# Earlier sinks for the second batch, first keys on a second queue, first query planes on two engines, wide masks behind them

## The chip, the cores and the metric
One core of one Trainium2 chip. The metric is device time in microseconds. The engines are TensorE (PE in the rows; PEld is its weight load), VectorE (DVE), ScalarE (ACT), GpSimd (POOL) and SyncE (SP), which here only issues DMAs. Each engine works through its own instructions in order.

## The reference
Sliding-window attention with four sink keys, and behind it a gated MLP with a short convolution:

```
scores = q @ k.T / 8;  keep = (key < n_sink) | (0 <= query - key < window)      # B=4, H=8, S=768, D=64
x   = softmax(where(keep, scores, -1e9)) @ v          # n_sink = 4, window = 128; heads joined: 512 columns
h   = relu(x @ w_in)                                  # 1024 columns
out = (h * sigmoid(conv3(h, conv_w))) @ w_out         # conv over the sequence, per column
```

q, k and v are float32; the MLP's weights come as float64, two words a number.

## The kernel before, in words
A short prelude loads the two scalars (number of sinks, window), starts the first loads, builds an identity and the tables of positions, and computes a flag; then all engines branch on it (L904 to L906). What follows is the fast path, `banded`; nothing of it starts before the branch.

Two heads make a pair `g`; four pairs make a batch of the input. A step `i` is one tile of 128 queries of one pair: 6 steps a pair, 24 a batch. The first batch goes in half pairs of three steps, in plain float32: `prep32` (L349) transposes three query tiles and three key tiles of the pair on TensorE; ScalarE writes the queries twice, as plane 0 and plane 1 (each with one head's rows scaled and the other's zero, by `headscale`), and then the keys. From the second batch on `prep` (L295) splits queries and keys into a high and a low part in the narrower matmul type; the low parts are staged in tiles of the tag "nat" (three buffers, `pieces_of`) and copied to their places by DMAs: `X<-bq` for queries, `kk<-bk` and `kk<-kk` for keys.

In each step `scores` multiplies (L378, or L381 and L382), VectorE adds the mask and takes the maximum (L577), ScalarE exponentiates (L580), VectorE sums and inverts (L583, L584), GpSimd scales (L586). One step later `transp` transposes the weights; later still `pv` multiplies them with v (L655) and adds the sinks' part (L678). Masks: `m0` for the first tile; `w1` and `w2` (wide, 260 columns) for the others of the first batch; `m1` and `m2` (narrow, 132 columns), made from the wide ones in `narrow_masks` (L484), for the later batches.

The sinks' values of the first batch lie in `c.vs`, inside a buffer of the keys, cleared by GpSimd behind the wide masks (L496) and loaded by `sink_load` (L416). Those of the later batches are fetched by `sink_fetch` (L426) into a "nat" tile, split by `sink_split` (L435: one instruction on ScalarE, three on VectorE) and copied to `vsr` by DMAs, two `vsr<-sink` and two `vsr<-vsr`. The fetch is written at a batch's first step, the split three steps later (L748 to L752).

The MLP's weights are fetched piece by piece (`wi_0r`, ..., also "nat" tiles), put together from their two words and split into two parts on ScalarE, VectorE and GpSimd (L118 to L131), all within the first batch. The MLP of a batch is cut into pieces that fill TensorE between the steps of the next one (L204 and L239).

A scheduler with its own cost model sets the order on each engine when the program is built. What is written inside `first` has a higher priority: scores, transposes, products and the preparation of later pairs. `follow` adds a dependence on another instruction. SyncE issues all DMAs but the very last.

Of the kernel before, what the change touches and what calls it, by code (L numbers as in the profile page):

```python
# [17 lines left out]
P = 128  # L18
D = 64
NEG = 1.0e9  # L20
NS = 4
# [45 lines left out]
class Moe:  # L67
# [31 lines left out]
    def load(self, src, name):  # L99
        nc, (rows, n) = self.c.nc, src.shape  # L100
        if src.dtype == F32:
            raw = self.mp.tile([P, 512], F32, tag="nat", name=f"{name}r", bufs=3)[0:rows, 0:n]
            nc.sync.dma_start(raw, src)
        else:
            raw = self.mp.tile([P, 512, 2], I32, tag="nat", name=f"{name}r", bufs=3)[0:rows, 0:n]
            nc.sync.dma_start(raw.rearrange("p n w -> p (n w)"), src.bitcast(I32))
        return raw
# [166 lines left out]
class Attn:  # L274
# [74 lines left out]
    def prep32(self, g, half, s, kk, tag, ahead):  # L349

        c, nc, T, HTL, kw = self.c, self.nc, self.T, self.HTL, self.kw
        tiles = slice(HTL * half, HTL * half + HTL)

        def turn(nm):
            pt = self.mps.tile([P, HTL, P], F32, tag=tag, name=f"tr{nm}{g}{half}", bufs=3 if tag == "h" else 2)
            for t in range(HTL):
                c.pin(nc.tensor.transpose(pt[:, t, :], s.raw[nm, half][:, t].rearrange("p a d -> p (a d)"), c.ident))
            if nm == "q":
                s.X[half] = f(self.ap.tile([P, 2, HTL, P], F32R, tag="X", name=f"X{g}{half}", bufs=3))
                for j in range(2):  # L360
                    self.evac(s.X[half][:, j], pt, c.headscale[:, j:j + 1])
            else:
                s.kk = kk
                self.evac(kk[:, tiles, 0:P], pt, 1.0)
                if half == 0:
                    nc.scalar.copy(kk[:, :, P:kw], kk[:, 0:1, 0:kw - P].to_broadcast([P, T, kw - P]))
            ahead()

        s.plain = True
        return [lambda nm=nm: turn(nm) for nm in "qk"]  # L370
# [19 lines left out]
        nc.vector.tensor_tensor(out=xL[:, hp, s], in0=px, in1=f(xH[:, hp, s]), op=ALU.subtract)  # L390


def load(c, g, nm, t, lo, hi):

    b, hp = divmod(g, c.H // 2)
    both = getattr(c, nm)[b, 2 * hp:2 * hp + 2]
    if nm == "v" and hi - lo == c.S // P:
        c.nc.sync.dma_start(t.rearrange("p j t d -> p (j t) d"), both.rearrange("j (t p) d -> p (j t) d", p=P))
        return t
    for j in range(2):  # L400
        c.nc.sync.dma_start(t[:, j] if nm == "v" else t[:, :, j], both[j].rearrange("(t p) d -> p t d", p=P)[:, lo:hi])
    return t


def load_half(c, g, nm, half, slot):
    n = c.S // P // 2
    return load(c, g, nm, slot, n * half, n * half + n)


def load_v(c, g, slot, lo=0, hi=None):  # L410
    hi = hi or c.S // P
    load(c, g, "v", c.v_raw[slot][:, :, lo:hi], lo, hi)
    return c.v_raw[slot]
# [37 lines left out]
def banded(c):  # L451
# [18 lines left out]
    nc.vector.tensor_tensor(out=m0, in0=inw, in1=sk, op=ALU.max)  # L470
    nc.vector.tensor_scalar(m0, m0, -NEG, NEG, ALU.mult, ALU.add)
    w1, w2 = wide
    nc.vector.tensor_scalar(w1[:, KW:SW], inw, -NEG, NEG, ALU.mult, ALU.add)
    nc.vector.tensor_scalar(w1[:, 0:P], prv, -NEG, NEG, ALU.mult, ALU.add)
    nc.vector.tensor_tensor(out=w1[:, P:KW], in0=sk[:, 0:NS], in1=prv[:, 0:NS], op=ALU.is_gt)
    nc.vector.tensor_scalar(w1[:, P:KW], w1[:, P:KW], -NEG, NEG, ALU.mult, ALU.add)
    nc.vector.tensor_copy(w2, w1)
    masks = nc.vector.tensor_scalar(w2[:, P:KW], sk[:, 0:NS], -NEG, NEG, ALU.mult, ALU.add)

    def afterwards(ins):  # L480
        c.tc.add_manual_dep(ins.ins, masks.ins.name, mybir.DependencyInfo(mybir.DependencyClass.Sync,
                                                                          mybir.DependencyReason.DATA), reason="masks")
# [1 line left out]
    def narrow_masks():  # L484
        for mk, w in ((m1, w1), (m2, w2)):
            ins = nc.scalar.copy(mk[:, 0:NS], w[:, P:KW])
            c.tc.add_manual_dep(ins.ins, c.turned.ins.name, mybir.DependencyInfo(mybir.DependencyClass.Sync,
                                                                                mybir.DependencyReason.DATA), reason="late")
            nc.vector.tensor_tensor(out=mk[:, NS:KW], in0=w[:, 0:P], in1=w[:, KW:SW], op=ALU.min)

    n0, n1 = T * KW, 3 * NPAIR * P
    A.zeros = m.room[0][:, 6 * SW:6 * SW + n0]
    afterwards(nc.gpsimd.memset(A.zeros, 0.0))
    kks = [f(ap.tile([P, 4, T, KW], F32R, tag="kk", name=f"kks{i}")) for i in range(2)]
    c.vs = kks[1].rearrange("p a t k -> p (a t k)")[0:6 * SP, 2 * n0:2 * n0 + n1].rearrange("p (u n) -> p u n", u=3)
    afterwards(nc.gpsimd.memset(c.vs, 0.0))  # L496
    vsr = cp.tile([3 * SR, 3, NPAIR * P], F32R, name="vsr")

    half_row = n1 // 2
# [210 lines left out]

    for x in prep(0):
        x()
    load_v(c, 0, 0, 0, T // 2)
    m.fetch(1)
    sink_load(c, 0)
    fetch()
# [17 lines left out]
    for i in range(NST + DL):  # L734
        if i < NST:
# [9 lines left out]
            if i == NSTB // 2:  # L745
                for x in range(0, 2 * half_row, half_row):
                    nc.sync.dma_start(f(vsr).rearrange("p u n -> p (u n)")[:, x:x + half_row], A.zeros[0:3 * SR, 0:half_row])
            if t == 0 and g and g % NPAIR == 0:  # L748
                sinks = sink_fetch(c, m, g // NPAIR)
                after = i + 3  # L750
            if i == after:
                sink_split(c, vsr, *sinks)  # L752
# [103 lines left out]
def attention_gated_mlp(ctx: ExitStack, tc: tile.TileContext, q, k, v, n_sink, window, w_in, conv_w, w_out, out):  # L856
# [11 lines left out]
    c.raw = [c.whole[i // 2][:, T // 2 * (i % 2):T // 2 * (i % 2 + 1)] for i in range(RAWB)]  # L868
    c.v_raw = [con.tile([P, 2, T, D], F32, name=f"vraw{i}") for i in range(2)]
    for i in range(RAWB):  # L870
        load_half(c, i // 2, "qk"[i % 2], 0, c.raw[i])
    fl = con.tile([P, 2], F32, name="fl")
    flag = con.tile([1, 1], I32, name="flag")
    nc.vector.tensor_scalar(fl[:, 0:1], c.wnv, 1.0, None, ALU.is_ge)
# [67 lines left out]
```

## Time and profile before

| | |
|---|---|
| time, median of 3 runs | 474.92 us (474.6 to 476.47) |
| profiled execution: time, span | 473.48 us, 471.8 us |
| granted clock of TensorE, mean | 0.997 |
| PE busy | 444.6 us (94%), 3181 instructions |
| PEld busy | 388.3 us (82%) |
| DVE busy | 339.0 us (72%) |
| ACT busy | 321.3 us (68%) |
| POOL busy | 281.3 us (60%) |
| first key and query loads | 96 KB each transfer, two transfers a half |
| a piece of w_in or w_out | 512 KB |

The span runs from the first to the last instruction. Busy time is that in which an engine has an instruction in work; waiting for a semaphore is not counted. A row that ends in brackets tells how long the engine idled before it and what released it; the releaser is inferred and can be wrong where several semaphores are waited for.

### The profile page before, as it was taken

Reading aid. Unit: us, or ns where it says so; the run is one execution under the profiler, and the core shown is the slowest. Engines: PE = TensorE matmul, PEld = TensorE weight load, DVE = VectorE, ACT = ScalarE, POOL = GpSimd, SP = SyncE. Lnnn points to the kernel's source line nnn. Section 1 sums busy time; section 2 is a strip of 40 time slices with the busy share of each in tenths; the row PEclk is TensorE's granted clock in tenths of the full one; section 3 lists DMA queues with packets and bytes.
Section 4 is the critical chain, followed back from the end, with each engine's and each line's share of the span. In section 5 each row is a group of like instructions: output and inputs, shape, how many; then the busy total and the mean of one; then the engine's idle time right before and its main releaser. Section 6 shows DMA issues by size and latency. Waiting matters only on the chain.

```text
span 471.8 us, 10560 instructions
## 1 busy us (share of the span) xinstructions
PE 444.6 (94%) x3181; PEld 388.3 (82%) x3181; DVE 339.0 (72%) x1190; ACT 321.3 (68%) x1027; POOL 281.3 (60%) x557
## 2 busy tenths in 40 slices
PE   3898989898899999999999999999999999999994
PEld 3576768697798988898989898988989898998982
DVE  4799999758858668786766859685767663665562
ACT  4989957768867868785867767675857654554542
POOL 3474786626858658676755757667656671445340
PEclk9999999999999999999999999999999999999998
DMA  6888674388667472655273655545250101000001
GB/s 140 219 229 251 183 201 107 81 199 203 167 153 179 137 175 68 161 146 133 61 192 81 166 119 134 143 120 124 71 141 15 46 1 46 0 23 24 24 24 53
DMA packets 105851, 55.91 MB, mean 119 GB/s; under 512 B 83072, under 2 KB 98712, under 8 KB 105784
## 3 DMA queue, kind: packets, MB, share of 16 engines
q1 hardware_dynamic: 105640, 55.00, 45.5%
q8 instruction: 28, 0.46, 0.4%
q14 instruction: 39, 0.32, 0.2%
q10 hardware_dynamic: 144, 0.13, 0.1%
HBM read 28.17 MB, written 6.29 MB: 73 GB/s over the span
## 4 chain that ended last, share of the span: by engine, by line
PE 75%; DVE 11%; ACT 4%; POOL 3%; DMA 2%; issue 2%; DVEq 0%; POOLq 0%; ACTq 0%
PE ph L204 26%; PE po L239 25%; PE px L655 7%; PE sc L382 3%; PE sc L381 3%; PE pts L617 3%; PE px L678 2%; DVE stm L122 2%; PE tq L305 1%; PE tk L331 1%; DVE stm L123 1%; DMA kk<-bk 1%; DMA raw<-in_q_dram 1%; DVE roomH L577 1%; DVE roomL L577 1%
## 5 line engine op out<-in xcount | busy, mean ns | idle before, releaser
L239 PE MATMUL po<-woH,g 128*128 128x512 f32 x384 | 138.2, 405 | 1.5 <-POOL g L226 0.8
L204 PE MATMUL ph<-xH,wiH 128*128 128x258 f32 (+1 forms) x384 | 110.7, 288 | 0.0
L204 PE MATMUL ph<-xL,wiH 128*128 128x258 f32 (+1 forms) x384 | 109.6, 286 | 0.0
L204 PE MATMUL ph<-xH,wiL 128*128 128x258 f32 (+1 forms) x384 | 109.1, 284 | 0.0
L226 POOL TENSOR_SCALAR g<-t 128x256 fp32r<-128x256 f32 x94 | 44.3, 472 | 74.5 <-DVE t L219 50.6
L586 POOL TENSOR_SCALAR pe<-pe,sm 128x132 f32<-128x132 f32 (+1 forms) x144 | 62.8, 447 | 37.7 <-DVE sm L584 19.2
L239 PEld LDWEIGHTS po<-woH,g 128*128 128x128 f32 x384 | 69.4, 189 | 13.2 <-POOL g L226 1.7
L227 POOL TENSOR_TENSOR g<-t,g 128x256 fp32r<-128x256 f32 x94 | 74.5, 793 | 5.8
L239 PE MATMUL po<-woL,g 128*128 128x512 f32 x192 | 76.1, 396 | 0.0
L216 DVE SCALAR_TENSOR_TENSOR t<-hb,cw,t 128x256 f32<-128x256 f32 x96 | 53.8, 560 | 29.4 <-ACT t L215 28.9
L204 PEld LDWEIGHTS ph<-xH,wiL 128*128 128x128 f32 x384 | 72.8, 190 | 2.2
L204 PEld LDWEIGHTS ph<-xH,wiH 128*128 128x128 f32 x384 | 72.7, 189 | 2.0
L204 PEld LDWEIGHTS ph<-xL,wiH 128*128 128x128 f32 x384 | 72.7, 189 | 1.6
L580 ACT ACTIVATE pe<-pe,sm 128x132 f32<-128x132 f32 (+1 forms) x144 | 58.2, 406 | 14.4 <-DVE sm L577 12.8
L218 ACT ACTIVATE t<-t 128x256 f32<-128x256 f32 x96 | 40.1, 418 | 36.3 <-DVE t L217 35.9
L219 DVE SCALAR_TENSOR_TENSOR t<-t,hb 128x256 f32<-128x256 f32 x96 | 48.3, 504 | 15.1 <-ACT t L218 14.3
L215 ACT ACTIVATE t<-hb,cw 128x256 f32<-128x256 f32 x96 | 49.0, 511 | 12.4 <-POOL g L227 10.1
L217 DVE SCALAR_TENSOR_TENSOR t<-hb,cw,t 128x256 f32<-128x256 f32 x96 | 54.4, 567 | 4.0 <-POOL pe L586 0.5
L211 ACT ACTIVATE hb<-ph 128x258 f32<-128x258 f32 (+1 forms) x96 | 36.8, 384 | 17.4 <-PE ph L204 13.9
L577 DVE CUSTOM_DVE_ANT_0 pe<-sc,m 128x132 f32<-128x132 f32 (+1 forms) x144 | 39.8, 287 | 7.7 <-PE sc L382 6.9
L381 PE MATMUL sc<-kk,X 128*128 128x260 f32 (+1 forms) x144 | 42.3, 304 | 1.5 <-issue 1.1
L655 PE MATMUL px<-pT,vraw 128*64 128x128 f32 (+1 forms) x512 | 43.0, 317 | 0.0
(161 smaller groups left out, 896.1 us busy)
## 6 DMA issues: line engine op xcount, KB each, us to landing
X<-bq SPq DMA_DIRECT2D x96, 96.0 KB
vraw<-in_v_dram SPq DMA_DIRECT2D x16, 384.0 KB
out_dram<-stm SPq DMA_DIRECT2D x23, 256.0 KB
kk<-kk SPq DMA_DIRECT2D x24, 198.0 KB
raw<-in_k_dram SPq DMA_DIRECT2D x24, 192.0 KB
raw<-in_q_dram SPq DMA_DIRECT2D x24, 192.0 KB
kk<-bk SPq DMA_DIRECT2D x48, 96.0 KB
raw<-in_q_dram SPq DMA_DIRECT2D x16, 96.0 KB
```

The source lines that it names most:

```text
L204: self.latest = nc.tensor.matmul(u.h[:, 0:W], w[:, cc, ff * P:(ff + 1) * P], x[:, cc, t0:t1], start=(i == 0), stop=(i == len(prods) - 1))
L215: nc.scalar.mul(a, prev, cw[:, 0, ff:ff + 1])
L216: nc.vector.scalar_tensor_tensor(out=e, in0=this, scalar=cw[:, 1, ff:ff + 1], in1=a, op0=ALU.mult, op1=ALU.add)
L217: nc.vector.scalar_tensor_tensor(out=a, in0=nxt, scalar=cw[:, 2, ff:ff + 1], in1=e, op0=ALU.mult, op1=ALU.add)
L219: nc.vector.scalar_tensor_tensor(out=a, in0=e, scalar=1.0, in1=this, op0=ALU.add, op1=ALU.mult)
L227: nc.gpsimd.tensor_tensor(out=u.g[:, 1], in0=a, in1=f(u.g[:, 0]), op=ALU.subtract)
L239: ins = nc.tensor.matmul(po[:, 0:c.DM], u.g[:, a, tt * P:(tt + 1) * P], w[:, ff, :], start=(ff == 0 and i == 0), stop=(ff == NFF - 1 and i ...
L381: self.c.pin(self.nc.tensor.matmul(pc, X[:, j, u, :], kk[:, j, lo:hi], start=True, stop=False))
L577: nc.vector.tensor_tensor_reduce(out=pe[:, j, cols], in0=pc[:, P - at:SW][:, cols], in1=mk, op0=ALU.add, op1=ALU.min, scale=1.0, scalar=3. ...
L580: exp = nc.scalar.activation(pe[:, j, cols], pe[:, j, cols], AF.Exp, bias=sm[:, j:j + 1], scale=-1.0, accum_out=sm[:, 2 + 2 * j:3 + 2 * j])
L586: nc.gpsimd.tensor_scalar(pe[:, j, cols], pe[:, j, cols], sm[:, 8 + j:9 + j], 1.0, ALU.mult, ALU.mult)
L655: ins = nc.tensor.matmul(px[h][D * j:D * j + D, P * at:P * at + n], s.v[:, j, kt, :], pT, start=(h not in open_), stop=False, skip_group_c ...
```

## The change
Five edits. The prelude issues the four first half loads from two queues, queries from SyncE's and keys from ScalarE's, and the first value load directly behind them, before the branch instead of after the first preparation. In the first preparation VectorE, not ScalarE, writes the second query plane (`c.moved`). The six instructions that make the wide masks, and the two clears behind them, are made to follow that. The two narrow masks' VectorE instruction is made to follow a late transpose (`c.turned`), as its ScalarE one did before. The second batch's sinks are fetched at step 21 instead of 24, and so split at 24 instead of 27; those of the third and fourth batch stay.

```diff
             if nm == "q":
                 for j in range(2):
-                    self.evac(s.X[half][:, j], pt, c.headscale[:, j:j + 1])
+                    if g == half == 0 and j:
+                        c.moved = nc.vector.tensor_scalar(s.X[half][:, j], pt, c.headscale[:, j:j + 1], None, ALU.mult)
+                    else:
+                        self.evac(s.X[half][:, j], pt, c.headscale[:, j:j + 1])
...
-def load(c, g, nm, t, lo, hi):
+def load(c, g, nm, t, lo, hi, by=None):
+    by = by or c.nc.sync
...
-        c.nc.sync.dma_start(t[:, j] if nm == "v" else t[:, :, j], both[j].rearrange("(t p) d -> p t d", p=P)[:, lo:hi])
+        by.dma_start(t[:, j] if nm == "v" else t[:, :, j], both[j].rearrange("(t p) d -> p t d", p=P)[:, lo:hi])
...
-    nc.vector.tensor_scalar(w1[:, KW:SW], inw, -NEG, NEG, ALU.mult, ALU.add)
-    nc.vector.tensor_scalar(w1[:, 0:P], prv, -NEG, NEG, ALU.mult, ALU.add)
...
-    masks = nc.vector.tensor_scalar(w2[:, P:KW], sk[:, 0:NS], -NEG, NEG, ALU.mult, ALU.add)
...
-            nc.vector.tensor_tensor(out=mk[:, NS:KW], in0=w[:, 0:P], in1=w[:, KW:SW], op=ALU.min)
+            ins = nc.vector.tensor_tensor(out=mk[:, NS:KW], in0=w[:, 0:P], in1=w[:, KW:SW], op=ALU.min)
+            follow(c, ins, c.turned, "late")
...
-    afterwards(nc.gpsimd.memset(A.zeros, 0.0))
-    afterwards(nc.gpsimd.memset(c.vs, 0.0))
...
     for x in prep(0):
         x()
-    load_v(c, 0, 0, 0, T // 2)
+    follow(c, nc.vector.tensor_scalar(w1[:, KW:SW], inw, -NEG, NEG, ALU.mult, ALU.add), c.moved, "masks later")
+    follow(c, nc.vector.tensor_scalar(w1[:, 0:P], prv, -NEG, NEG, ALU.mult, ALU.add), c.moved, "masks later")
...
+    masks = nc.vector.tensor_scalar(w2[:, P:KW], sk[:, 0:NS], -NEG, NEG, ALU.mult, ALU.add)
+    afterwards(nc.gpsimd.memset(A.zeros, 0.0))
+    afterwards(nc.gpsimd.memset(c.vs, 0.0))
     m.fetch(1)
     sink_load(c, 0)
...
-            if t == 0 and g and g % NPAIR == 0:
-                sinks = sink_fetch(c, m, g // NPAIR)
+            if i == NSTB - 3 or t == 0 and g > NPAIR and g % NPAIR == 0:
+                sinks = sink_fetch(c, m, max(1, g // NPAIR))
                 after = i + 3
...
     for i in range(RAWB):
-        load_half(c, i // 2, "qk"[i % 2], 0, c.raw[i])
+        load_half(c, i // 2, "qk"[i % 2], 0, c.raw[i], nc.scalar if i % 2 else nc.sync)
+    load_v(c, 0, 0, 0, T // 2)
```

## Rows read from the trace of the kernel before

**Rows 1.** Busy us (instructions) by stretch: PE, PEld, DVE, ACT, POOL; clock, DMA share, GB/s.
```profile
42.00:84.00 42.00, 37.54 (x277) 31.07 (x277) 41.83 (x110) 32.26 (x90) 27.45 (x36) 1.00 0.63 170
...
90.00:108.00 18.00, 18.00 (x158) 16.26 (x157) 10.88 (x41) 13.48 (x43) 6.50 (x13) 1.00 0.81 194
108.00:114.00 6.00, 5.33 (x44) 5.02 (x44) 5.93 (x27) 5.52 (x22) 3.21 (x8) 1.00 0.97 230
...
120.00:126.00 6.00, 4.80 (x30) 3.85 (x29) 5.13 (x28) 4.40 (x19) 5.30 (x12) 1.00 0.47 141
126.00:456.00 330.00, 329.59 (x2384) 293.90 (x2382) 229.79 (x815) 220.55 (x719) 204.68 (x413) 1.00 0.39 99
```

**Rows 2.** The chain of waits at the start: start us, us, what.
```profile
8.27 4.86 DMA raw<-in_q_dram
...
13.62 0.87 PE trq L357 x3
```

**Rows 3.** SyncE's queue at the start, in order of time: start us, us, issue.
```profile
1.25 0.42 SPq L57 DMA_DIRECT2D sc_i<-in_window_dram  x1
...
6.66 0.91 SPq L401 DMA_DIRECT2D vraw<-in_v_dram  x2
7.68 0.42 SPq L106 DMA_DIRECT2D wi_0r<-in_moe_w_in_dram  x1
8.27 0.90 SPq L401 DMA_DIRECT2D raw<-in_q_dram  x2
```

**Rows 4.** The engines at the start, in order of time.
```profile
4.79 0.17 DVE L59 CAST sc_f<-sc_i 128x4 f32<-128x4 int32 x1 [2.78 <-DMA sc_i<-in_window_dram]
...
6.91 0.88 PE L357 MATMUL trq<-ident,raw 128*128 128x128 f32 x3 [6.91 <-SPq L938]
...
7.90 1.05 ACT L288 ACTIVATE X<-trq,headscale 128x384 f32<-128x384 f32 x2 [1.93 <-DVE roomH L474]
...
10.71 0.29 DVE L577 CUSTOM_DVE_ANT_0 roomH<-sc,m 128x128 f32<-128x128 f32 x1 [1.60 <-PE sc L378]
...
12.89 0.66 ACT L118 ACTIVATE stm<-wi_0r 128x512 f32<-128x512 f32 x1 [0.48 <-DMA wi_0r<-in_moe_w_in_dram]
...
14.51 1.05 ACT L288 ACTIVATE X<-trq,headscale 128x384 f32<-128x384 f32 x2 [0.47 <-PE trq L357]
```

**Rows 5.** Busy time by stretch again, the first loads.
```profile
4.50:7.00 2.50, 0.10 (x1) 0.13 (x2) 1.96 (x10) 0.20 (x1) 0.38 (x11) 1.00 1.07 241
```

**Rows 6.** The masks: roomH's instructions by stretch (DVE fourth); L489's durations.
```profile
7.33:9.20 1.87, 0.00 (x0) 0.00 (x0) 1.46 (x8) 0.00 (x0) 0.23 (x1) 1.00 0.82 136
...
L489 DVE TENSOR_TENSOR m<-roomH x2: 286/288/289, 8.0 to 8.8; 128x128 f32<-128x128 f32 x2
```

**Rows 7.** The sinks' tile alone, by stretch: DVE, ACT, clock, DMA share, GB/s.
```profile
108.00:114.00 6.00, 1.88 (x3) 0.60 (x1) 1.00 0.97 230
```

**Rows 8.** SyncE's queue at the second batch's start.
```profile
101.99 1.14 SPq L431 DMA_DIRECT2D sink<-in_v_dram  x3
...
112.53 0.54 SPq L344 DMA_DIRECT2D kk<-kk  x1
...
118.23 1.79 SPq L446 DMA_DIRECT2D vsr<-sink  x2
120.12 1.41 SPq L340 DMA_DIRECT2D kk<-bk  x2
121.63 1.67 SPq L448 DMA_DIRECT2D vsr<-vsr  x2
```

**Rows 9.** Who waited for whom, 90 to 127 us: us, times, longest.
```profile
PE tk L637 <- DVE sk L629: 0.7, 1, 0.7
...
PE sc L381 <- issue: 1.1, 1, 1.1
...
ACT kk L342 <- DMA kk<-bk: 1.6, 1, 1.6
```

**Rows 10.** ScalarE at the fifth pair's second query half.
```profile
96.66 0.50 ACT L288 ACTIVATE bq<-tq 128x384 fp32r<-128x384 f32 x1
```

More of the change, by code (lines that the diff above doesn't have):

```diff
@@ L400, in load, with load_half @@
     for j in range(2):
-        c.nc.sync.dma_start(t[:, j] if nm == "v" else t[:, :, j], both[j].rearrange("(t p) d -> p t d", p=P)[:, lo:hi])
+        by.dma_start(t[:, j] if nm == "v" else t[:, :, j], both[j].rearrange("(t p) d -> p t d", p=P)[:, lo:hi])
     return t
-def load_half(c, g, nm, half, slot):
+def load_half(c, g, nm, half, slot, by=None):
     n = c.S // P // 2
-    return load(c, g, nm, slot, n * half, n * half + n)
+    return load(c, g, nm, slot, n * half, n * half + n, by)
 def load_v(c, g, slot, lo=0, hi=None):
@@ L472, in banded @@
     w1, w2 = wide
-    nc.vector.tensor_scalar(w1[:, KW:SW], inw, -NEG, NEG, ALU.mult, ALU.add)
-    nc.vector.tensor_scalar(w1[:, 0:P], prv, -NEG, NEG, ALU.mult, ALU.add)
-    nc.vector.tensor_tensor(out=w1[:, P:KW], in0=sk[:, 0:NS], in1=prv[:, 0:NS], op=ALU.is_gt)
-    nc.vector.tensor_scalar(w1[:, P:KW], w1[:, P:KW], -NEG, NEG, ALU.mult, ALU.add)
-    nc.vector.tensor_copy(w2, w1)
-    masks = nc.vector.tensor_scalar(w2[:, P:KW], sk[:, 0:NS], -NEG, NEG, ALU.mult, ALU.add)
     def afterwards(ins):
@@ L712, in banded @@
         x()
-    load_v(c, 0, 0, 0, T // 2)
+    follow(c, nc.vector.tensor_scalar(w1[:, KW:SW], inw, -NEG, NEG, ALU.mult, ALU.add), c.moved, "masks later")
+    follow(c, nc.vector.tensor_scalar(w1[:, 0:P], prv, -NEG, NEG, ALU.mult, ALU.add), c.moved, "masks later")
+    follow(c, nc.vector.tensor_tensor(out=w1[:, P:KW], in0=sk[:, 0:NS], in1=prv[:, 0:NS], op=ALU.is_gt), c.moved, "masks later")
+    follow(c, nc.vector.tensor_scalar(w1[:, P:KW], w1[:, P:KW], -NEG, NEG, ALU.mult, ALU.add), c.moved, "masks later")
+    follow(c, nc.vector.tensor_copy(w2, w1), c.moved, "masks later")
+    masks = nc.vector.tensor_scalar(w2[:, P:KW], sk[:, 0:NS], -NEG, NEG, ALU.mult, ALU.add)
+    afterwards(nc.gpsimd.memset(A.zeros, 0.0))
+    afterwards(nc.gpsimd.memset(c.vs, 0.0))
     m.fetch(1)
```

## The prediction

> **What bounds the kernel now.** I read the table of busy time by stretch first. From 126 us to 456 us TensorE is busy in 329.59 of 330 us [rows 1]: whatever reaches 126 us sooner ends sooner by as much, and nothing behind 126 us can be won. Ahead of it TensorE idles 0 in 90 to 108 us, 0.67 us in 108 to 114 and 1.20 us in 120 to 126, and in 42 to 84 us it is VectorE that is full (41.83 of 42 us) [rows 1]. So there are two places to look at: the start, because what delays VectorE's first work delays the whole first batch, and the entry into the second batch at 108 to 126 us. The chain of waits, read second, says what ends the start: the third query load, 4.86 us after its issue, and then its transposes at 13.62 us [rows 2]. SyncE's queue, third, says why that load is late: the first value load (0.91 us of issuing) and the weight piece wi_0r are issued ahead of it, from 6.66 us on, when the branch into the fast path has been taken [rows 3]. The engines' rows, fourth, give the branch itself: VectorE reads the window size at 4.79 us after waiting for its load, TensorE begins at 6.91 us, and ScalarE evacuates the first query planes, two in 1.05 us, from 7.90 us [rows 4]. For the second batch I read SyncE's queue and the waits.
>
> **The loads.** Two key halves leave SyncE's queue for ScalarE's, and the value load moves ahead of the branch, right behind the queries. ScalarE has nothing but the table load and one tiny activation until 7.90 us, so four issues cost it nothing. On SyncE the block's first issue is then wi_0r, at 6.66 instead of 7.68 us: 1.02 us sooner [rows 3]. The third query load still needs its buffer, free when the first query transposes are done (6.91 + 0.88 = 7.79 us [rows 4]), so it is issued some 0.4 us sooner; but it stands behind the 512 KB of wi_0r on the same 16 DMA engines, so its landing follows wi_0r's. I take 1.0 us sooner at the transposes of 13.62 us. Can ScalarE use that? It now idles 0.48 us for wi_0r at 12.89 us [rows 4], and it gets work out of its way by the next part, so it can. The bounds are 0 (ScalarE, not the load, is late) and 1.5 us (0.52 us of work and its waits of 0.48 and 0.47 us [rows 4] all gone).
>
> A load added beside the two scalar loads can also cost. The window size was issued at 1.25 us and read at 4.79 us [rows 3, 4]; now keys come from a second queue to the same engines meanwhile. Four key transfers of 96 KB at the 241 GB/s that 4.5 to 7 us shows, with the engines full [rows 5], are 1.6 us: the flag, and with it everything behind the branch, could be that much later. Or 0, if its few packets are through before the keys'. I take 0.2 us, near the lower end: the queries issued right behind it from 1.71 us on shared the engines with it before, too. The Trainium skill, DMA: Bandwidth & Descriptors, "Issuing engines are not separate DMA queues", says that loads started by different engines interleave on the same 16 DMA engines and that a second issuer saves only the issuing time; no row here shows two queues at once, and by that rule alone the keys gain no bandwidth and the scalar loads do share.
>
> **The first planes.** The second of the two evacuations goes to VectorE: 0.52 us less on ScalarE, whose first key evacuation and first scores come that much sooner. VectorE has the room: it waits 1.60 us for the first scores at 10.71 us [rows 4]. This is not added to the 1.0 us; it lets ScalarE take that. If both planes were still done one behind the other, the buffer would be free at 9.0 us as now, and the second group's transposes would gain nothing.
> The Trainium skill, PSUM — Partial Sum Buffer, "PSUM bank collisions raise a hardware error", wants accesses of ScalarE and VectorE to one bank kept apart, reads too; no row here shows the two on one PSUM tile at once. By it the second plane would start behind the first, the start would gain some 0.8 us instead of 1.0, and the sum below would be 1.7 us.
>
> **The masks.** The wide masks move behind that evacuation: six instructions, which with the two narrow ones are 1.46 us busy [rows 6]. They fit into VectorE's 1.60 us wait, late by about 0.9 us, and so are the two clears behind them on GpSimd and the six sink loads on SyncE. Those loads are first read with the products of the first sinks, steps later; cost 0 to 0.9 us, taken 0 for that cover; if it were gone, those products would wait the 0.9 us. The two narrow masks (0.29 us each [rows 6]) are now tied to a late transpose and leave this idle stretch for the neighbourhood of 85 us, where VectorE is still the one behind: 0 to 0.58 us, taken 0.3.
>
> **The sinks of the second batch.** Fetch, split and copies move three steps ahead. In 108 to 114 us VectorE is busy 5.93 of 6 us [rows 1] and 1.88 us of it are the sinks' three instructions, with 0.60 us on ScalarE [rows 7]; three steps sooner, in 90 to 108 us, VectorE is busy 10.88 of 18 us [rows 1]. So that part is free where it goes. What it frees: TensorE's wait of 0.7 us for VectorE's sk [rows 9] should vanish, but what TensorE needs next is the sixth head pair's keys, whose last copies are issued at 112.53 us [rows 8] and which hang on the end of the first batch (the buffer), not on the sinks; TensorE then only waits there longer. I take 0.2 us of the 0.7 and of the 1.1 us for the scores behind it [rows 9], between all of it, 1.8, and nothing.
> On SyncE's queue the two vsr<-sink issues take 118.23 to 120.02 us, and the seventh pair's low keys, kk<-bk, issue at 120.12 [rows 8]; ScalarE then idles 1.6 us for them [rows 9], and TensorE's 1.20 us in 120 to 126 us follow. With the 1.79 us gone from there that wait and those gaps should be gone: 1.2 us. Bounds 0 (another transfer takes the place) and 1.2.
> Where they go, SyncE has them ahead of the sixth pair's keys: the fetch (1.14 us) leaves 101.99 us for the idle queue before, but copies of 1.79 and 1.67 us come in: 3.46 - 1.14 = 2.3 us more at worst ahead of 112.53 us [rows 8], 0 at best, if they fall into the hole that the fetch leaves and others like it. I take 0, nearer to it, because the copies that remain are split by a landing and need not stand together; the 0.2 above is net of it.
>
> **The sum.** 1.0 - 0.2 - 0.3 + 0.2 + 1.2 = 1.9 us less. The profiled execution took 473.48 us (span 471.8), so 471.6 us on its scale. It lies 1.44 us below the median shown, 474.92 us, so I forecast 474.92 - 1.9 = 473.0 us.
>
> **The rivals.**
> 1. All gaps of the second batch's entry close: 1.2 us and the whole 1.8 us instead of 0.2, and the start gains its 1.0 without the deductions: 1.2 + 1.8 + 1.0 = 4.0 us, 470.9 us. For it: VectorE and SyncE both get freer at 108 to 120 us. Against: the sixth pair's keys are a chain of transfers that the change does not shorten.
> 2. The entry gains nothing: the keys at 120 us wait for another issue in the place of vsr<-sink, and only the start is left, 0.5 us: 474.4 us. For it: from 118.23 to 123.30 us the queue has no hole [rows 8]. Against: ScalarE's wait of 1.6 us is just as long as the two issues.
> 3. Slower. The sinks share three buffers with the low parts of keys and queries. Fetched at about 85 us, they hold one until vsr<-sink has landed; the second query half of the fifth pair, evacuated by ScalarE at 96.66 us [rows 10], can be given that buffer. ScalarE works in order, so behind its wait stand the exponentials and the copies of transposes, and TensorE behind these. The sinks held their buffer 18 us, from 101.99 to 120.02 us [rows 8]; from 85 us that would be 103 us, a wait of some 6.4 us at 96.66. Less the gain of 1.9 us it is 4.5 us more: 479.4 us; it decides from a wait of 1.9 us on. Against: of three buffers the sinks may as well hold one that nobody wants until they are through; no row of before can show which.
> 4. The change's first part backfires: the flag is 1.6 us late by the keys' traffic. Then 1.9 - 1.4 = 0.5 us is left of the gain: 474.4 us, no slower.
>
> **Chances.** Forecast 0.44 (its own range 472.0 to 474.2, about a quarter of it below 472.5), rival 1 0.27, rivals 2 and 4 together 0.17, rival 3 0.12. What one measurement can tell here from no change is about 0.5%, 2.4 us: below 472.5 us is faster, above 477.3 slower. Faster: 0.27 and 0.11 of the forecast's, 0.38. Slower: most of rival 3, 0.10. The same: 0.52. The range goes from 470.2 us (rival 1 with another 0.5 us, up to the start's bound of 1.5, and 0.2 us for the spread of the runs) to 476.4 us (rival 3 with a wait of 3.4 us).
>
> **What would show it.** Right: wi_0r issued at 6.7 us, the third query's transposes at about 12.6 us, VectorE's plane beside ScalarE's; vsr<-sink issued before 110 us; no wait of ScalarE for kk<-bk at 123 us, and TensorE idle under 0.3 us in the 6 us around it. Wrong: TensorE's first transposes later than 7.2 us (the flag); ScalarE waiting before a query evacuation near 96 us (the buffer); or over 1.8 us of TensorE's idling before the sixth pair's first scores, which would mean that the sinks' copies stand in front of its keys.

## The result, and the profile after

The changed kernel is slower. It takes 478.99 us (median of 14 runs, 476.72 to 483.67) against 474.28 us for the kernel before (14 runs, 472.78 to 477.12): a ratio of 1.0105, with a 95% interval of 1.0079 to 1.0131. That is 4.7 us more, outside the predicted range. The profiled execution took 479.68 us with a span of 478.0 us. Of the runs of the experiments below, two slow ones (1523 us of e5, 480.9 us of e15) are left out of the ratios.

On the page of the changed kernel, the line of TensorE's busy time and, in 40 slices of 11.95 us, the clock that it was granted:

```profile
PE 448.7 (94%) x3181; PEld 390.4 (82%) x3181; DVE 339.3 (71%) x1191; ACT 320.3 (67%) x1026; POOL 279.9 (59%) x557
...
PEclk9989999998999999999999999999999999999998
```

The 3181 matmuls are the same as before, yet they keep TensorE busy for 4.1 us more than the 444.6 us of before. Three slices of the clock stand at 8: the last, as before, and the third and the tenth, which were at 9 before. The busy time by stretch (PE, PEld, DVE, ACT, POOL, then clock, DMA share, GB/s) shows it closer:

```profile
24.00:26.00 2.00, 1.84 (x4) 1.40 (x5) 1.49 (x7) 1.21 (x8) 2.00 (x5) 0.54 0.82 214
26.00:28.00 2.00, 2.00 (x21) 1.62 (x21) 2.00 (x8) 1.47 (x5) 1.10 (x2) 0.61 0.87 270
...
114.00:116.00 2.00, 0.21 (x2) 0.24 (x3) 0.92 (x3) 1.61 (x6) 0.00 (x0) 1.00 0.90 205
116.00:118.00 2.00, 2.00 (x12) 2.00 (x12) 1.63 (x9) 2.00 (x9) 1.18 (x3) 0.58 1.05 278
118.00:120.00 2.00, 2.00 (x12) 2.00 (x11) 1.30 (x5) 0.77 (x3) 1.92 (x4) 0.57 0.64 163
120.00:126.00 6.00, 6.00 (x43) 5.41 (x42) 4.02 (x16) 4.82 (x17) 4.66 (x11) 1.00 0.59 159
126.00:456.00 330.00, 327.04 (x2362) 290.72 (x2361) 231.16 (x829) 220.45 (x723) 202.39 (x413) 1.00 0.39 100
```

The clock stood at 1.2 GHz, half of 2.4, twice for 3.4 us, from 24.2 us and from 116.3 us; the second time right behind a stretch in which TensorE worked for 0.21 of 2 us. Matmuls for 6.8 us at half speed cost some 3.4 us. From 126 to 456 us TensorE idles for 2.96 us, against 0.41 before [rows 1].

TensorE's last matmul ends 5.5 us later than before. That is 4.1 us of busy time, 0.2 us of later start and, as the difference, 1.2 us of idling. The idling did not grow ahead of 126 us; the first two rows are of the kernel before, the others of the changed one:

```profile
0.00:126.00 126.00, 105.75 (x756) 87.40 (x757) 104.44 (x366) 96.21 (x300) 74.60 (x142) 1.00 0.69 179
108.00:126.00 18.00, 15.07 (x104) 13.10 (x104) 15.17 (x73) 14.50 (x56) 13.67 (x28) 1.00 0.69 176
```

```profile
0.00:126.00 126.00, 106.87 (x743) 87.80 (x744) 99.91 (x347) 92.55 (x287) 72.56 (x137) 0.97 0.67 178
108.00:126.00 18.00, 16.09 (x110) 15.18 (x109) 11.82 (x49) 13.44 (x49) 9.37 (x21) 0.91 0.77 193
```

Up to 126 us TensorE idles 1.1 us less than before (19.13 us for 20.25), and 1.0 us of that lies at the entry into the second batch (1.91 us for 2.93). So the profile's loss is 3.4 us of half clock, some 0.7 us of other busy time and 2.55 us of idling behind 126 us, less these 1.1 us.

The start, answering to [rows 3] and [rows 4] (start us, us, engine line, what, and in brackets the idle time before):

```profile
4.98 0.17 DVE L59 CAST sc_f<-sc_i 128x4 f32<-128x4 int32 x1 [2.96 <-DMA sc_i<-in_window_dram]
6.85 0.34 SPq L106 DMA_DIRECT2D wi_0r<-in_moe_w_in_dram  x1
7.10 0.87 PE L357 MATMUL trq<-ident,raw 128*128 128x128 f32 x3 [7.10 <-SPq L942]
7.31 0.36 SPq L106 DMA_DIRECT2D wi_1r<-in_moe_w_in_dram  x1
8.00 0.91 SPq L405 DMA_DIRECT2D raw<-in_q_dram  x2
8.10 0.58 ACT L288 ACTIVATE X<-trq,headscale 128x384 f32<-128x384 f32 x1 [1.94 <-DVE m L475]
8.78 0.62 DVE L362 TENSOR_SCALAR X<-trq,headscale 128x384 f32<-128x384 f32 x1 [0.71 <-ACT X L288]
...
12.90 0.65 PEld L357 LDWEIGHTS trq<-ident,raw 128*128 128x128 f32 x3 [0.32 <-ACT kks L369]
13.11 0.85 PE L357 MATMUL trq<-ident,raw 128*128 128x128 f32 x3
```

The second batch's start in SyncE's queue, answering to [rows 8]: first the sixth pair's keys in the kernel before, then the changed kernel, and below it the changed kernel's chain of waits over the same time:

```profile
106.18 3.02 SPq L340 DMA_DIRECT2D kk<-bk  x4
```

```profile
103.47 1.78 SPq L450 DMA_DIRECT2D vsr<-sink  x2
...
106.54 1.57 SPq L452 DMA_DIRECT2D vsr<-vsr  x2
...
110.12 3.19 SPq L340 DMA_DIRECT2D kk<-bk  x4
...
115.32 0.54 SPq L344 DMA_DIRECT2D kk<-kk  x1
...
122.51 1.28 SPq L340 DMA_DIRECT2D kk<-bk  x2
```

```profile
110.18 0.56 SPq L340
110.74 0.05 issue
110.79 3.50 DMA kk<-bk
114.29 0.02 issue
114.31 0.04 ACTq L342
114.35 0.04 issue
114.39 0.27 ACT kk L342
114.66 0.40 ACT bq L288
115.06 0.02 issue
115.08 0.57 DVE bq L310
115.65 0.14 issue
115.79 4.29 PE ph L204 x21
```

The sixth pair's keys (kk<-bk) are issued behind the sinks' copies, and the landing of these keys is what TensorE waits for: ScalarE, in order, can't evacuate the query behind its wait for kk, VectorE can't make bq, and TensorE stands still for 1.91 us until 115.79 us. What it then begins with are matmuls of the MLP (ph L204); the sixth pair's first scores come behind these. That is the last sign on the prediction's list of wrong ones. The waits of 90 to 127 us, answering to [rows 9], no longer have TensorE waiting for sk; ScalarE's wait for the keys is this one:

```profile
ACT kk L342 <- DMA kk<-bk: 2.2, 1, 2.2
```

### The profile page after: what moved, and what is told of

The parts are those of the page before. It is cut to its first block, busy times and chain, and to the rows that moved or that the text cites. A ratio compares the mean times of both kernels' runs of the same rounds, so it can differ in the third digit from the quotient of the medians.

```text
span 478.0 us, 10559 instructions
## 1 busy us (share of the span) xinstructions
PE 448.7 (94%) x3181; PEld 390.4 (82%) x3181; DVE 339.3 (71%) x1191; ACT 320.3 (67%) x1026; POOL 279.9 (59%) x557
## 4 chain that ended last, share of the span: by engine, by line
PE 76%; DVE 7%; ACT 5%; POOL 4%; issue 2%; DMA 2%; SPq 1%; POOLq 0%; ACTq 0%; DVEq 0%
PE ph L204 27%; PE po L239 26%; PE px L651 7%; PE sc L385 3%; PE sc L384 3%; PE pts L613 3%; PE px L674 2%; PE tk L331 1%; PE sc L381 1%; PE tq L305 1%; POOL roomH L582 1%; POOL roomL L582 1%; ACT stm L118 1%; DVE stm L122 1%; DMA kk<-bk 1%
## 5 line engine op out<-in xcount | busy, mean ns | idle before, releaser
L204 PE MATMUL ph<-xH,wiH 128*128 128x258 f32 (+1 forms) x384 | 112.6, 293 | 1.9 <-DVE bq L310 1.9
L204 PE MATMUL ph<-xL,wiH 128*128 128x258 f32 (+1 forms) x384 | 110.5, 288 | 0.0
L204 PE MATMUL ph<-xH,wiL 128*128 128x258 f32 (+1 forms) x384 | 110.2, 287 | 0.0
L226 POOL TENSOR_SCALAR g<-t 128x256 fp32r<-128x256 f32 x94 | 42.5, 452 | 69.2 <-DVE t L219 42.4
L216 DVE SCALAR_TENSOR_TENSOR t<-hb,cw,t 128x256 f32<-128x256 f32 x96 | 55.9, 583 | 36.2 <-ACT t L215 35.8
L204 PEld LDWEIGHTS ph<-xH,wiH 128*128 128x128 f32 x384 | 73.5, 191 | 4.2 <-issue 2.1
L227 POOL TENSOR_TENSOR g<-t,g 128x256 fp32r<-128x256 f32 x94 | 73.1, 778 | 5.5
L204 PEld LDWEIGHTS ph<-xH,wiL 128*128 128x128 f32 x384 | 73.4, 191 | 2.1
L204 PEld LDWEIGHTS ph<-xL,wiH 128*128 128x128 f32 x384 | 73.3, 191 | 1.7
L217 DVE SCALAR_TENSOR_TENSOR t<-hb,cw,t 128x256 f32<-128x256 f32 x96 | 50.7, 529 | 3.9 <-DVE t L216 0.5
L572 DVE COPY_PREDICATED sc<-before,sc 128x128 f32<-128x128 int32 x120 | 33.3, 289 | 17.4 <-PE sc L385 17.0
L617 POOL TENSOR_SCALAR_AFFINE_SELECT pT<-pT 128x256 f32<-128x256 f32 x60 | 27.1, 452 | 28.4 <-ACT pT L615 26.1
## 6 DMA issues: line engine op xcount, KB each, us to landing
raw<-in_k_dram SPq DMA_DIRECT2D x24, 192.0 KB
raw<-in_q_dram SPq DMA_DIRECT2D x24, 192.0 KB
```

The source lines that it names most:

```text
L204: self.latest = nc.tensor.matmul(u.h[:, 0:W], w[:, cc, ff * P:(ff + 1) * P], x[:, cc, t0:t1], start=(i == 0), stop=(i == len(prods) - 1))
L216: nc.vector.scalar_tensor_tensor(out=e, in0=this, scalar=cw[:, 1, ff:ff + 1], in1=a, op0=ALU.mult, op1=ALU.add)
L217: nc.vector.scalar_tensor_tensor(out=a, in0=nxt, scalar=cw[:, 2, ff:ff + 1], in1=e, op0=ALU.mult, op1=ALU.add)
L226: nc.gpsimd.tensor_scalar(u.g[:, 0], a, 1.0, 1.0, ALU.mult, ALU.mult)
L227: nc.gpsimd.tensor_tensor(out=u.g[:, 1], in0=a, in1=f(u.g[:, 0]), op=ALU.subtract)
```

## The experiments

All are compared with the kernel before in runs on the same chip (median 473.7 to 474.3 us). "Clock" is the mean granted clock over all runs of the kernel (0.996 for the kernel before, 0.990 for the changed one), "idle" TensorE's idle time in 126 to 456 us of its profile (before 0.41, changed 2.96 us). "List" tells which order of matmuls TensorE's list of instructions has from the program's 1200th matmul (in the trace at 212 us before) to the 2400th (388 us), where all lists meet again: a as before, b as in the changed kernel, c to f others; e10's list is d from 221 us on, and that of e14 and e16 is b from 250 us on. The order is made by the scheduler that builds the program (the planner, below), so an edit anywhere can give another list.

| | edit | us | ratio, 95% interval | clock | idle | list |
|-|-|-|-|-|-|-|
| e1 | sinks sooner | 477.4 | 1.0065, 1.0037 to 1.0093 | 0.994 | 1.78 | c |
| e2 | loads | 474.9 | 1.0009, 0.9989 to 1.0028 | 0.991 | 1.06 | d |
| e3 | planes, masks, tie | 478.6 | 1.0083, 1.0053 to 1.0113 | 0.993 | 2.80 | b |
| e4 | all but the sinks | 478.0 | 1.0073, 1.0040 to 1.0106 | 0.991 | 0.70 | a |
| e5 | planes, wide masks | 474.8 | 1.0022, 1.0000 to 1.0045 | 0.992 | 0.40 | a |
| e6 | tie alone | 480.2 | 1.0136, 1.0103 to 1.0168 | 0.992 | 1.88 | b |
| e7 | e1, copies by GpSimd | 477.7 | 1.0073, 1.0043 to 1.0102 | 0.997 | 4.45 | e |
| e8 | sinks fetched sooner | 474.3 | 1.0005, 0.9982 to 1.0028 | 0.996 | 0.41 | a |
| e9 | changed, split later | 480.7 | 1.0143, 1.0121 to 1.0165 | 0.986 | 0.77 | a |
| e10 | changed, tie sooner | 477.7 | 1.0081, 1.0053 to 1.0108 | 0.991 | 1.50 | d |
| e11 | e1, tie one step sooner | 476.1 | 1.0045, 1.0026 to 1.0064 | 0.993 | 0.86 | a |
| e12 | tie three steps sooner | 477.1 | 1.0064, 1.0049 to 1.0079 | 0.992 | 0.76 | a |
| e13 | e2, filled | 476.8 | 1.0046, 1.0024 to 1.0067 | 0.993 | 0.43 | d |
| e14 | narrow masks later, free | 474.4 | 1.0006, 0.9983 to 1.0029 | 0.997 | 0.75 | f, then b |
| e15 | e4 without tie, filled | 476.1 | 1.0025, 0.9997 to 1.0052 | 0.992 | 0.43 | d |
| e16 | e14 with the tie | 475.1 | 1.0033, 1.0009 to 1.0056 | 0.994 | 0.47 | f, then b |
| e17 | keys by ScalarE | 475.1 | 1.0014, 0.9994 to 1.0033 | 0.996 | 0.44 | a |
| e18 | parts that leave the list | 475.1 | 1.0025, 1.0004 to 1.0046 | 0.992 | 0.42 | a |

**The parts, e1 to e4.** e1 is the kernel before with the changed lines of the sinks; e2 with those of the loads; e3 with the second plane, the wide masks and the tied narrow masks; e4 is the changed kernel with the sinks at their old place.

```
 e1  -  if t == 0 and g and g % NPAIR == 0:
     +  if i == NSTB - 3 or t == 0 and g > NPAIR and g % NPAIR == 0:
 e2  +  load_half(..., nc.scalar if i % 2 else nc.sync); load_v(c, 0, 0, 0, T // 2)
 e3  +  c.moved = nc.vector.tensor_scalar(...); follow(c, <wide masks>, c.moved, ...)
     +  follow(c, ins, c.turned, "late")     (narrow masks)
 e4  the changed kernel with "if t == 0 and g and g % NPAIR == 0:"
```

> Before, with only the second batch's sinks three steps sooner. Theory K (the sinks' copies stand in SyncE's queue ahead of the sixth pair's keys; TensorE waits 1.9 us for them and its clock then falls to half for 3.4 us): the same wait near 115 us and the fall behind it, so 1.0 to 1.9 us of wait + 1.7 us of clock, less the 1.2 us gained behind: ratio 1.003 to 1.007. Theory S (the loss is made at the start, by the loads, planes and masks): no loss here, ratio 0.995 to 1.000. Theory P (any edit changes the order on all engines and so the fill of TensorE): a loss anywhere, TensorE idle spread over the later batches.

> Before, with only the loads moved (keys by ScalarE's queue, first values before the branch). K: the start gains up to 0.5 us, nothing lost: ratio 0.998 to 1.000. S: a fall of the clock near 24 us as in the changed kernel, 1.7 us, ratio 1.003 or more. P: a loss with another order, idle spread.

> Before, with only the second query plane on VectorE and the masks behind it (wide and narrow). K: ratio 0.998 to 1.001. S: loss of 1 to 3 us before 45 us, with a fall of the clock near 24 us, ratio 1.003 to 1.006. P: as in the others, a loss behind 126 us.

> The changed kernel with the sinks where they were. K: the wait of 1.9 us near 115 us and the fall of the clock behind it are gone: 3.6 us less than the changed kernel, ratio to before 1.000 to 1.004. S: the start's loss stays, ratio 1.006 to 1.010.

e1 shows the sinks' copies in front of the keys: the gap ahead of the sixth pair's first scores is 2.04 us, for 1.05 before, with kk<-kk at its end.

```profile
116.95 0.30 PE L381 MATMUL sc<-kk,X 128*128 128x128 f32 x1 [2.04 <-DMA kk<-kk]
```

The loads alone cost nothing that can be measured. The surprise is e3: the part that the prediction had at 0.3 us costs 4 us. And the parts don't add up: 0.1 + 0.7 + 0.8% is more than the 1.05% of all together, and without the sinks the kernel is nearly as slow as with them: e4's ratio lies in the range of theory S, not of K.

**The masks and the sinks taken apart, e5 to e8.** e5 is e3 without the tie, e6 the tie without the rest of e3. e7 is e1 with the four copies in another queue, e8 moves only the fetch.

```
 e6     ins = nc.vector.tensor_tensor(out=mk[:, NS:KW], ..., op=ALU.min)
     +  follow(c, ins, c.turned, "late")
 e7  -  nc.sync.dma_start(dst, src)           (sink_split, all four)
     +  nc.gpsimd.dma_start(dst, src)
 e8     as e1, but   after = NSTB + 3 if i < NSTB else i + 3
```

> The kernel before with the second query plane on VectorE and the wide masks behind it, but the narrow masks' minima left free, as before. In the order of the instructions this moves 6 rows of TensorE's list against the kernel before; with the tie (the third experiment) 634 rows move. Theory T (the tie of the narrow masks makes the planner order everything behind it anew, and the loss of the third experiment is that new order): 472.5 to 475.0 us, within 0.3% of the kernel before, and in the profile under 1.2 us of TensorE idle between 126 us and the end, as before (0.28 and 0.64). Theory S (the first 30 us are worse with the plane and the masks, and that is carried along): 477 to 479 us.

> The kernel before with the two minima of the narrow masks tied to the last turned keys, and nothing else. 628 rows of TensorE's list stand elsewhere, although the four instructions tied last 1.2 us on VectorE in all. Theory T: 477 to 479 us, as the third experiment (478.6), with TensorE idle for 2 to 3.5 us between 126 us and the end, and a gap of about 1.0 us near 192 us. Theory S: 474 to 475 us, as the kernel before, since nothing changes in the first 30 us.

> The kernel before with the sinks three steps sooner (as in the first experiment, 477.4 us), and their four copies into vsr issued by GpSimd's queue instead of SyncE's, for every batch. Theory K (the copies stand in front of the sixth pair's keys in SyncE's queue): the gap of 2.0 us ahead of the sixth pair's first scores falls to 1.1 us or less, and the time is 474 to 475.5 us. Theory P (it is the new order of everything behind that costs, not the queue): the gap may go, but the time stays at 476.5 to 478 us, with the idle time at other places behind 126 us. If GpSimd waits at the copies, its gates come late and the second matmuls of the experts wait for them: over 478 us.

> The kernel before with the sinks' three loads from memory issued three steps sooner, and their split and copies where they were before. TensorE's list is the same row by row; 6 rows of SyncE's list move. Theory K: nothing that TensorE waits for changes: 473.5 to 474.8 us, the gap ahead of the sixth pair's first scores stays at 1.1 us. If the loads from memory were what made the sixth pair's keys late, not the copies: the gap grows to about 2 us and the time to 476 us or more. If the sinks' tile, held for three steps longer, starves the other users of its buffers: 476 us or more with other gaps between 87 and 118 us.

e5 and e6 put the loss of e3 on the tie, and e8 puts that of e1 on the split and copies. e7 tells the queue from the rest. Its stretches (columns as above):

```profile
108.00:114.00 6.00, 6.00 (x51) 5.86 (x51) 4.40 (x22) 5.72 (x23) 3.71 (x10) 1.00 0.92 189
114.00:120.00 6.00, 6.00 (x42) 5.40 (x42) 5.52 (x22) 5.55 (x20) 5.25 (x13) 1.00 0.62 154
120.00:126.00 6.00, 5.55 (x43) 4.87 (x43) 4.30 (x16) 4.07 (x16) 4.89 (x10) 1.00 0.99 267
126.00:456.00 330.00, 325.55 (x2343) 288.77 (x2340) 227.47 (x814) 218.08 (x713) 205.30 (x414) 1.00 0.38 97
```

With the copies out of SyncE's queue the entry into the second batch is closed, as the prediction's first rival wanted: TensorE idles 0.45 us from 108 to 126 us. That and the chain of waits above put the gap on the queue, though e7's list is another one, too (e for c). Yet the time does not fall, because 4.45 us of idling now stand behind 126 us.

**Is it one order? e9 to e12.** I took the loss for that of one order of TensorE's list. e9 to e12 bring other orders into the slow kernels by shifting one edit by a step or three.

```
 e9  the changed kernel,   after = NSTB + 1 if i < NSTB else i + 3
 e10 the changed kernel,   if i == NSTB - 6:  narrow_masks()     (was NSTB - 3)
 e11 e1 with the tie,      if i == NSTB - 4:  narrow_masks()
 e12 e6,                   if i == NSTB - 6:  narrow_masks()
```

> The changed kernel with the sinks fetched three steps sooner, as there, but split and copied one step later than there (two steps sooner than in the kernel before). TensorE's list stands behind its thousandth row again as in the kernel before (the changed kernel, and the first, third, sixth and seventh experiment, all share another order there, which I call order X). Theory T (order X costs 2 to 4 us in the second batch): 475 to 476.5 us, and in the profile under 1 us of TensorE idle between 130 and 456 us. Theory S or K (the losses were made in front of that: the start, the sinks' copies ahead of the sixth pair's keys): 477.5 to 479.5 us.

> The changed kernel with the narrow masks made three steps sooner and nothing else. The sinks' copies stand in front of the sixth pair's keys in SyncE's list as in the changed kernel; behind the thousandth row TensorE's list stands as in the second experiment (the loads alone, 474.9 us), so it isn't order X. Theory T: 475 to 477 us, with 1.0 to 1.5 us of idle left in front of the sixth pair's keys. Theory K (the copies and what follows them are the loss): 478 to 480 us, as the changed kernel.

> The kernel before with the sinks three steps sooner, all of it as in the first experiment, and the narrow masks tied and made one step sooner, by which TensorE's list stands as before behind its thousandth row. The sinks' copies are ahead of the sixth pair's keys. It gives the price of the queue alone: theory T and K together say a gap of about 2 us (1.05 before) ahead of the sixth pair's first scores and 474.5 to 476 us; theory T alone, with the gap made up for behind it: 473.5 to 474.5 us; if the sinks cost by themselves whatever the order: 477 to 478 us as in the first experiment.

> The kernel before with the narrow masks tied as in the sixth experiment (480.2 us), but made three steps sooner. The same two minima wait for turned keys; TensorE's list stands as before behind its thousandth row. Theory T: 473.5 to 475 us. If the tied minima cost by themselves (VectorE late at the step that it works at, wherever that is): 477 to 480 us.

Two things in these texts were wrong. Matmul by matmul, only the changed kernel, e3 and e6 share an order there; e1 and e7 have their own (c, e). And the lists that are said to stand as before, or as in e2, behind the thousandth row do so only behind the 1200th matmul or so. The theory foretold the idle time behind 126 us, which fell to 0.76 to 0.86 us with list a and 1.50 us with d. It failed on the time: e9 is the slowest of all, e11 lies 0.1 us above its range, and e12's 477.1 us lies in the range given for a tie that costs by itself. One thing it had left out is the clock: e9's mean is 0.986, and its profile has 3.4 us at half clock from 119.3 us, behind a gap of 1.78 us; e12's has one from 125.7 us, at the end of a gap of 2.44 us.

**Clock and order by themselves, e13 to e16.** e13 and e15 issue the transposes of the first two pairs' probabilities twice, into the same tile. e14 makes the narrow masks one step later and untied; e16 adds the tie to e14.

```
 e13, e15  +  for again in range(2 if g < 2 else 1):
                  c.pin(nc.tensor.transpose(pt[:, w, j, :], ...))
 e14, e16  -  if i == NSTB - 3:  narrow_masks()
           +  if i == NSTB - 2:  narrow_masks()
```

> The second experiment (the loads alone: 474.9 us, mean granted clock 0.991) with the transposes of the first two pairs' probabilities issued twice, 44 matmuls more of 0.12 us or so, into the same tile with the same result. TensorE's list behind its thousandth row stands as in the second experiment. Theory C (TensorE's clock falls after idle places near 24 us, and each fall costs about 1.7 us): the mean granted clock rises to 0.994 or more and the time falls to 472.5 to 474 us, below the kernel before. If the falls don't hang on idle places there: clock 0.991 and 475 to 476 us.

> The kernel before with the narrow masks made one step later and not tied: the same instructions, no wait added. In rows 1200 to 2400 of TensorE's list it has the changed kernel's order, matmul by matmul, and in 400 rows ahead of that an order of its own. Theory T (this order costs by itself): 476.5 to 479 us at a mean clock near 0.995, and over 2 us of TensorE idle between 126 and 456 us. If what costs is the work that the other kernels moved, not the order: 473.5 to 475 us.

> The changed kernel with the sinks at their old place, the narrow masks not tied, and the transposes of the first two pairs' probabilities issued twice. Behind the thousandth row TensorE's list stands as in the second experiment. Theories T and C together: 472.5 to 474.5 us. If the start's edits cost by themselves (the fourth experiment, 478.0 us, has the same start): 476 to 479 us.

> The fourteenth experiment (474.4 us) with the two minima of the narrow masks tied to the last turned keys. The lists of TensorE, ScalarE and GpSimd are the same row by row; on VectorE the two minima stand some 230 rows further back, and nothing else. If the tie costs by its wait (as the sixth experiment, 480.2 us, might be read): 477 to 480 us. If it costs only through the order that the planner makes of everything else: 474 to 475 us.

e13 lies outside both of its ranges. e15 missed the first of its two and lies at the lower edge of the second, that of a start which costs by itself. The fall at 24 us is gone from e13's profile, but the doubled work made a new list and with it a new gap, and the clock fell there (the first row is TensorE's, the others are stretches):

```profile
63.98 0.75 PE L239 MATMUL po<-woH,g 128*128 128x512 f32 x1 [1.99 <-POOL g L226]
```

```profile
62.00:64.00 2.00, 0.01 (x1) 0.02 (x1) 2.00 (x5) 1.80 (x5) 1.93 (x4) 1.00 0.78 237
64.00:68.00 4.00, 4.00 (x28) 3.12 (x28) 4.00 (x13) 2.10 (x6) 3.87 (x5) 0.57 0.54 150
```

e14 shows that a new list is not a loss as such: about as many matmuls stand elsewhere as in e6 and nothing measurable is lost. Its text claims list b from the 1200th matmul; by the traces it is b only from 250 us on. So the order behind 250 us is cleared, but the stretch ahead of that is not: the changed kernel, e3 and e6, whose lists agree from 178 us of the changed kernel on, all stall in it (e6's row below, TensorE waiting for GpSimd's gate g; 1.01 us at 192.0 us in the changed kernel and 1.00 in e3), and e14 does not.

```profile
189.57 0.50 PE L239 MATMUL po<-woH,g 128*128 128x512 f32 x1 [1.01 <-POOL g L226]
```

e16 clears the tie as a wait: with e14's lists of TensorE, ScalarE and GpSimd it takes 1.45 us more than the kernel before where e14 takes 0.49 (medians): about 1 us for the tie, not 6. The traces say the same of the other kernels with the tie, e12 among them: in all nine VectorE goes from the instruction ahead straight to the two minima, without idling, and these take 0.55 to 0.79 us. In e6:

```profile
85.87 0.71 DVE L489 TENSOR_TENSOR m<-roomH 128x128 f32<-128x128 f32 x2
```

**What is left of the change, e17 and e18.** e17 issues the first keys by ScalarE and nothing else. e18 has all that leaves the list alone: these keys, the plane and wide masks of e5, the fetch of e8.

```
 e17 +  load_half(c, i // 2, "qk"[i % 2], 0, c.raw[i], nc.scalar if i % 2 else nc.sync)
 e18 e17 + e5 + e8
```

> The kernel before with the first keys issued by ScalarE's queue, and the first values' load left at its old place. The lists of TensorE, VectorE and GpSimd stay as they were, row by row. If the loads' own gain is there (third query transposes some 0.5 to 1 us sooner, TensorE's start 0.2 us later), and the falls of the clock in the second experiment came with its new order: 473.0 to 474.3 us with a mean clock of 0.995. If they came with the loads: 474.5 to 475.5 us with a mean clock near 0.991.

> All the parts of the change that leave TensorE's list as it was (12 rows of difference in the first 200, none behind): the first keys by ScalarE's queue, the second query plane on VectorE, the wide masks behind it, the sinks fetched three steps sooner; without the values' earlier load, the tie of the narrow masks and the sooner split. If the order was what cost: 473 to 475 us, the mean clock deciding (the fifth experiment, with the planes and wide masks, had 0.992 and 474.8 us). If the parts cost by themselves: over 476 us.

Neither costs over 0.5% and neither gains. In its profiled execution e18 had a clock of 0.999 and took 473.2 us, but its mean over the runs is 0.992 and its median 475.1 us. No version beat the kernel before.

## Why the prediction was wrong

Three steps failed. Two had no term in the sum: TensorE's clock (some 3.4 us in the profile) and the idling behind 126 us (2.55 us more). The third was taken at 0: the sinks' copies in SyncE's queue (0.9 us). What the sum did contain came out in part: 1.1 us less idling ahead of 126 us for a forecast 1.9.

**A step that failed: "I take 0" for SyncE's queue.** The prediction had bounds of 0 and 2.3 us for the sinks' copies ahead of the sixth pair's keys, and took 0, since they "need not stand together". They need not: it is enough that they are ahead. 1.78 + 1.57 us of copies come in ahead of the keys and the fetch of 1.14 us leaves: 2.2 us, about the upper bound. The keys' issue moved by more, 3.9 us, from 106.18 us before to 110.12 us; what the rest is, is not shown. TensorE's gap there is 1.91 us for 1.05 before; e1 has it alone at 2.04 us, and e7, with the copies out of the queue, not at all. So the term measured 0.9 us in TensorE's time. This is the smallest of the three: with the 1.2 us that the prediction won behind it the entry still idles 1.0 us less than before. What made the entry dear is the fall of the clock right behind the gap, some 1.7 us; that the gap brought it on is not shown, since e1's gap has none behind it.

**"Nothing behind 126 us can be won" was read as "nothing can be lost".** The sum has no term for it: it took each instruction's order outside the moved ones as given. The planner makes the order of all engines anew, and TensorE's full 329.59 of 330 us [rows 1] hangs on the list: with a the profiles have 0.40 to 0.86 us of idling there, with d 0.43 to 1.50 and with b 1.88 to 2.96. The changed kernel has 2.55 us more than before; e1, e3, e6 and e7 have 1.4 to 4.0 us more, by e7 even with the entry closed.

**The clock was not in the sum at all.** It is at 1.00 in every row shown of before [rows 1], so there was a price to ask for: what happens to it when a gap grows. The same four score matmuls, at the same place of the same list, in the changed kernel and then in e4:

```profile
24.16 2.10 PE L381 MATMUL sc<-kks,X 128*128 128x260 f32 x4 [0.40 <-DVE sm L573]
```

```profile
24.04 1.15 PE L381 MATMUL sc<-kks,X 128*128 128x260 f32 x4 [0.40 <-DVE sm L573]
```

The 0.95 us between them is the clock alone. In the profiled execution the two falls are the largest single part of the loss, 3.4 us. Over all runs of all these kernels, each against its own kernel's mean, the time rises by 3.2 us for each 0.01 by which the mean clock is lower (310 runs, correlation -0.72). The changed kernel's 0.990 for 0.996 is by that estimate 1.8 us of the 5.4 us between the two means, so that the clock's share lies somewhere between these two figures. It is not the whole loss: four runs of the changed kernel had a clock of 0.995 to 0.998, as the kernel before has, and took 476.7 to 477.9 us, on average 3.3 us above the mean of all runs of before (474.15 us). Of these 3.3 us the profile shows only a part as idling.

**The tie of the narrow masks, taken at 0.3 us.** By itself it is worth about 1 us at most (e16 against e14), and it makes VectorE wait for nothing. Added to the kernel before it costs 6 us (e6) by what comes with it, another list and a lower clock; that a list moved as far need not cost anything shows e14's, which was made without the tie. In the changed kernel the tie does nothing to the list of TensorE: the program built without it has the same one. So the prediction's 0.3 us may be right there; no run measured it.

**What was right, or half right.** The window size is read 0.19 us later (forecast 0.2). The third query's transposes come at 13.11 us, 0.5 us sooner for a forecast 1.0. By the profile they wait last for ScalarE (kks L369), 0.3 us, and no longer for the load, which is the case that the prediction had at its lower bound; two weight pieces, wi_0r and wi_1r, now stand ahead of that load, and whether this costs anything is not shown. Before, too, the chain of waits had 0.47 us of another load (kks<-in_v_dram) between that load's landing at 13.13 us and the transposes, which the prediction did not count. The two planes are evacuated one behind the other, not side by side as forecast: VectorE begins at 8.78 us, 0.10 us after ScalarE's end. The Trainium skill, PSUM — Partial Sum Buffer, "PSUM bank collisions raise a hardware error", wants such accesses kept apart, and here they are. TensorE's wait for sk is gone. The last term, 1.2 us at the seventh pair's keys, is met: TensorE is busy for 6.00 of the 6 us from 120 us, and ScalarE's wait there is gone. It only came behind a gap and 3.4 us at half clock. Rival 3 didn't happen: at 94 to 99 us ScalarE waits for no query buffer.

**What stays open.** How much of the loss each part makes: e4, e9, e11 and e12 have list a and at most 0.45 us more idling behind 126 us than before, and still lose 2.3 to 6.9 us, by their medians. The clock explains a part: four runs of e4 at a clock of 0.994 to 0.997 took 475.2 to 476.7 us, still 1.9 us above the mean of before on average. Their lists ahead of 212 us differ from that of before, and no experiment separates that stretch. Open, too, is why the changed kernel stalls at 165 to 192 us, and which single row of its list does it: the lists of VectorE, ScalarE and GpSimd differ there too, and no experiment changed one of them alone. Nor is it shown what decides whether the clock falls: of 13 gaps of over 1.6 us between 10 and 130 us in the profiles of the changed kernel and the experiments, 11 have a fall beside them, e1's (2.04 us) and e18's (1.81 us) have none, and the changed kernel's fall at 24.2 us stands behind gaps of 0.46 us and less. It is one of six falls in that stretch of the profiles that have no such gap beside them. And e6's profiled execution, 476.9 us, is the fastest of its six, so the trace shows half of what it loses.

## What to carry to other kernels

Where a planner orders the instructions, price an edit by the list that it makes as well as by its own instructions: compare the two lists, and count a part that leaves the bottleneck's list alone as nearly free and one that rewrites it as worth anything from nothing to some microseconds more, in particular when the old list has the bottleneck full. In an in-order DMA queue, moving small copies sooner moves whatever is behind them later; look up which of those issues a full engine waits for before taking the cost as nothing. A gap on TensorE can cost twice, once as a gap and once as the clock behind it: a fall stood beside 11 of 13 gaps of over 1.6 us here, though the clock also fell without such a gap. Where such falls differ from run to run, read the time beside the mean clock.

## What the hardware showed

The falls of the clock to 1.2 GHz last 3.4 us in most of the profiles (6.8 us in e2's and e3's, 10.2 us in e10's) and are not the same from run to run of one kernel: the 14 runs of the changed kernel have mean clocks from 0.983 to 0.998, and the five at 0.983 to 0.986 are the five slowest (481.2 to 483.7 us). A second queue's four key issues, 2.09 us of ScalarE's time at the start, delayed the window size's load on the first queue by 0.19 us. TensorE's first matmul comes at 7.09 to 7.16 us in all nine profiles with the keys on ScalarE's queue, and at 6.85 to 6.92 us in the eleven others. The Trainium skill, DMA: Bandwidth & Descriptors, "Issuing engines are not separate DMA queues", has two issuers share the same 16 engines; the 0.19 us agree with that.
